# A list scheduler's cost table is refitted: attention and two MLPs in one kernel, same operations, another order

## The chip, the cores and the metric

The kernel runs on one core of a Trainium2 chip. The metric is the device time of one execution in microseconds (us), lower is better; the times shown are medians over several runs. A core has a matrix engine (TensorE, PE in the rows; PEld is its loading of weights), VectorE (DVE), ScalarE (ACT), GpSimd (POOL) and SyncE (SP). Here SP does nothing but issue transfers (DMA) between the chip's memory and the core.

## The reference

Three stages follow one another, with the output of each the input of the next. All tensors are fp32.

```python
# attention: q, k, v are (4, 8, 576, 64); window = 64
scores = scale * q @ k^T;  where not (0 <= pos_q - pos_k < window): -1e9
attn = exp(scores - max);  attn = attn / (sum + 1e-9);  out = attn @ v
x = out as 2304 tokens x 512
# first MLP: w_in (512, 2048), w_out (2048, 512), s and b scalars
r = max(x @ w_in, 0);  x = (s * r * r + b) @ w_out
# second MLP: w_in, w_out of the same sizes, alpha (2048,)
h = x @ w_in;  out = (max(h, 0) + alpha * min(h, 0)) @ w_out
```

## The kernel before, in words

Every fp32 matrix is split into a high and a low half, which PE multiplies as fp32r; one product costs three passes (high-high, high-low, low-high). Tokens lie along the columns.

In the opening, attention runs over groups of heads, block of tokens by block: scores on PE (L488, L500), mask and row maximum on DVE (L525), exponentials on ACT (L539), the sum's reciprocal on DVE (L549, L550), the normalising multiply on POOL (L557) or DVE, transposes (L574) and the product with v (L605) on PE. Between the groups, PE works on the first six of the first MLP's sixteen slices of 128 hidden units (L1075 in, L1135 out; 512 columns each). Later groups of heads lie beside that work, up to about 150 us.

The rest of the first MLP and all of the second work on pairs of slices and on thirds of the tokens, two halves of 384 columns, by a scheme with seven products in place of eight. Such a pair takes 90 matmuls of 384 columns: the products into the hidden units are L945, those out of them L1158. Copies of partial sums on ACT (L956) and one add on DVE (L973) stand between the L945 products; then comes the activation (ACT L1022 and L1026 in the first MLP, L1041 and L1042 with DVE L1045 in the second), the cast to the high half (ACT L1010 or DVE L1011) and the low half (DVE L1015). DVE adds the result onto the output (L1207).

The tokens' seven combinations (the X tiles, 768 KB each) are kept in the chip's memory and loaded for every turn by SP (L911). A weight slice is loaded by SP (L640, 512 KB), and prepared: two steps on ACT (L644, L648), five instructions on DVE (L653, L654, L658, L663 and the low half L675 or L711), the high half on ACT or DVE (L670, L672, L708). Three buffers hold loaded slices. The weight pairs' combinations are stored by SP (L758, wd<-ag) and loaded again for later turns (L779, aw<-wd).

No order is written out by hand. A class `Plan` collects 3475 steps, each with one or more ways (an engine, a cost in us, a function, a tail), the steps that it depends on and a due time `at`; some have an earliest time `after`. The method `emit` is a list scheduler that runs when the program is built: it keeps a time at which each engine comes free, computes for each ready step the earliest start (the end of what it depends on, plus `hop`, a cost for the change of engine), takes the earliest, and then among those of the same engine that could start then the one with the earliest due time:

```python
value = t + w[1] * (1.0 + self.SPARE[w[0]]) + w[3]   # the way taken is the one with the least
t0, i0, b0 = min(cands, key=lambda c: (c[0], self.steps[c[1]][2], c[1]))
```

So the costs decide two things: the order in which the steps stand on each engine, and, for steps with several ways, the engine. On the chip each engine runs its row in order, and waits for what its next instruction needs. Due times are worked out from absolute figures and from `PAIR`, the time of one pair of slices; `HURRY` (12 us) and `AHEAD` (30 us) set how far in front of its use a step is due or may begin.

Of the kernel before, what the change touches and what calls it, by code (L numbers as in the profile page):

```python
# [9 lines left out]
F32 = mybir.dt.float32  # L10
# [14 lines left out]
HALF = 384  # L25
# [43 lines left out]
class Plan:  # L69
# [93 lines left out]
    def emit(self):  # L163
# [67 lines left out]
def tile_window_attention_two_mlps(  # L231
# [78 lines left out]
    def dma(n, nbytes, fn):  # L310
        return [("sp", max(n * 0.45, nbytes / 380e3), fn, 2.0)]
# [18 lines left out]
    PAIR = 90 * (0.0137 + HALF * 0.00041)  # L330
# [5 lines left out]
    with tc.manual_schedule():  # L336
# [92 lines left out]
        def group(gi, bi, hps, at1, at2):  # L429
# [44 lines left out]
            def before():  # L474
# [30 lines left out]
                for t in range(len(hps)):  # L505
                    T.step([("pe", 0.25 + np_ * 0.23, lambda t=t: scores(t), 0.0)], reads=[(qk_, t)], writes=sc, at=at1)
# [37 lines left out]
                for h in range(2):  # L544
                    T.step([("act", 0.39 * NP, lambda h=h: exps(h), 0.1)], reads=[nm] + (sc if summed else [sm]),
# [6 lines left out]
                T.step([("dve", 0.36, inverse, 0.0)], writes=[(den, 0), (den, 1)], at=at1)  # L552
# [12 lines left out]
            def after():  # L565
# [10 lines left out]
                for h in range(2):  # L576
                    T.step([("pe", 0.05 + NP * 0.109, lambda h=h: transposes(h), 0.0)],
# [32 lines left out]
                for t in range(len(hps)):  # L610
                    T.step([("pe", 0.3 / len(hps) + 0.118 * u, lambda t=t: values(t), 0.0)],
# [18 lines left out]
        def converted(layer, f, part, at, after):  # L630
# [13 lines left out]
                [act(512, lambda: nc.scalar.activation(T[t], H().bitcast(F32), AF.Abs, scale=65536.0))],  # L644
# [3 lines left out]
                [act(512, lambda: nc.scalar.activation(L(), L().bitcast(U32), AF.Copy, scale=2.0 ** -29))],  # L648
# [7 lines left out]
            T.step([("dve", 0.8, exponent, 0.0, True)], writes=[t], at=at, after=after)  # L656
# [704 lines left out]
```

## Time and profile before

| | us |
|---|---|
| median of 3 runs | 852.15 |
| lowest, highest | 851.51, 853.44 |
| the profiled execution, device time | 854.11 |
| its span in the trace | 852.3 |
| PE busy | 832.7 |
| DVE busy | 651.1 |
| ACT busy | 510.5 |
| POOL busy | 103.5 |

A span is the time from the first to the last instruction in the trace; the device time of the same execution is 1.81 us longer. The busy time of an engine is the sum of its instructions' times. Idle time of an engine that isn't the bottleneck costs nothing by itself; it matters where the busiest engine waits for it.

### The profile page before, as it was taken

How to read it: one execution, taken by the hardware profiler on the slowest of the kernel's cores; microseconds unless marked ns; L12 is line 12 of the kernel's file. 1: busy time of each engine (PE TensorE's matmuls, PEld its weight loads, DVE VectorE, ACT ScalarE, POOL GpSimd, SP SyncE). 2: the span in 40 equal slices, each digit the busy share in tenths (PEclk: the TensorE clock that was granted, in tenths of full speed). 3: DMA queues.
4: the chain of work that ended last, by engine and by line, in shares of the span. 5: the costliest groups of instructions: out<-in, count | busy, mean ns of one | idle time of the engine just before them, and what ended most of it. 6: DMA issues, size and time to landing. Idle time of an engine off the chain costs nothing.

```text
span 852.3 us, 14883 instructions
## 1 busy us (share of the span) xinstructions
PE 832.7 (98%) x5556; PEld 787.7 (92%) x5556; DVE 651.1 (76%) x1175; ACT 510.5 (60%) x1217; POOL 103.5 (12%) x113
## 2 busy tenths in 40 slices
PE   7799999999999999999999999999999999999997
PEld 4678788888899999899999999999999999999997
DVE  6878799797997794699588989867767975864554
ACT  6878997545676474466365667655554754543431
POOL 6543344432100010011000000000000000000000
PEclk9999999999999999999999999999999999999999
DMA  8676973567578979957689359629774769435822
GB/s 282 195 214 179 297 229 111 209 218 275 202 253 316 406 243 363 380 189 305 225 319 340 131 214 354 239 75 346 259 252 156 243 254 348 144 110 187 295 76 75
DMA packets 65592, 202.57 MB, mean 238 GB/s; under 512 B 6640, under 2 KB 25072, under 8 KB 65520
## 3 DMA queue, kind: packets, MB, share of 16 engines
q1 hardware_dynamic: 65520, 201.62, 66.5%
q8 instruction: 44, 0.72, 0.3%
q14 instruction: 28, 0.23, 0.1%
HBM read 143.66 MB, written 57.93 MB: 237 GB/s over the span
## 4 chain that ended last, share of the span: by engine, by line
PE 88%; DMA 5%; ACT 2%; POOL 2%; DVE 1%; issue 1%; SPq 0%; DVEq 0%; POOLq 0%; ACTq 0%
PE y L1158 38%; PE h L945 18%; PE ab L945 13%; PE h L1075 9%; PE y L1135 4%; PE y L605 2%; DMA wd<-ag 2%; DMA raw<-w_out 2%; PE y L574 2%; PE ab L500 1%; DMA raw<-w_in 1%; POOL as__89 L557 1%; ACT as__89 L539 1%; PE ab L1158 0%; PE h L1158 0%
## 5 line engine op out<-in xcount | busy, mean ns | idle before, releaser
L1158 PE MATMUL y<-ax,woh 128*128 128x384 f32 x1216 | 275.4, 334 | 0.4 <-DVE ay L1207 0.4
L1158 PEld LDWEIGHTS y<-ax,woh 128*128 128x128 f32 x1216 | 216.3, 188 | 1.2 <-DVE ay L1207 0.9
L945 PE MATMUL h<-ax,aw 128*128 128x384 f32 x936 | 185.3, 335 | 0.3 <-ACT r L1022 0.2
L1158 PE MATMUL y<-ax,wol 128*128 128x384 f32 x608 | 169.4, 334 | 0.0
L945 PEld LDWEIGHTS h<-ax,aw 128*128 128x128 f32 x936 | 164.2, 188 | 1.4 <-ACT r L1022 0.6
L945 PE MATMUL ab<-ax,aw 128*128 128x384 f32 x702 | 140.4, 335 | 2.0 <-ACT h L956 1.5
L945 PEld LDWEIGHTS ab<-ax,aw 128*128 128x128 f32 x702 | 123.1, 188 | 2.9 <-ACT h L956 1.8
L1158 PEld LDWEIGHTS y<-ax,wol 128*128 128x128 f32 x608 | 111.1, 188 | 0.0
L1015 DVE TENSOR_TENSOR ax<-r,ax 128x384 fp32r<-128x384 f32 x156 | 86.2, 559 | 9.6 <-ACT ax L1010 7.5
L1207 DVE TENSOR_TENSOR ay<-y,ay 128x384 f32<-128x384 f32 x116 | 60.3, 552 | 38.5 <-PE y L1158 38.4
L1075 PE MATMUL h<-ax,aw 128*128 128x512 f32 (+1 forms) x360 | 85.1, 380 | 0.8 <-DVE ax L623 0.6
L1075 PEld LDWEIGHTS h<-ax,aw 128*128 128x128 f32 x360 | 62.8, 192 | 12.9 <-DVE ax L623 1.0
L1045 DVE SCALAR_TENSOR_TENSOR r<-aq,nalpha,r 128x384 f32<-128x384 f32 x96 | 58.5, 613 | 19.6 <-ACT aq L1042 16.6
L644 ACT ACTIVATE wt<-raw 128x512 f32<-128x512 f32 x64 | 43.3, 678 | 37.1 <-DMA raw<-w_out 16.3
L973 DVE TENSOR_TENSOR aq<-ab,aq 128x768 f32<-128x768 f32 x39 | 37.3, 956 | 31.1 <-PE ab L945 29.1
L1010 ACT CAST ax<-r 128x384 fp32r<-128x384 f32 x83 | 42.6, 514 | 25.9 <-DVE r L1045 23.7
L1041 ACT ACTIVATE r<-aq 128x384 f32<-128x384 f32 x48 | 24.8, 517 | 45.8 <-DVE aq L973 45.8
L658 DVE SCALAR_TENSOR_TENSOR raw<-raw 128x512 int32<-128x512 int32 x64 | 47.1, 738 | 1.8 <-ACT raw L648 1.8
L1026 ACT ACTIVATE r<-r 128x384 f32<-128x384 f32 (+2 forms) x90 | 47.5, 542 | 1.1
L557 POOL TENSOR_TENSOR as__89<-as__89,den 128x512 f32<-128x512 f32 x36 | 40.6, 1148 | 56.2 <-DVE den L550 43.7
L648 ACT ACTIVATE raw<-raw 128x512 int32<-128x512 uint32 x64 | 42.9, 679 | 5.7 <-DMA raw<-w_in 4.2
L663 DVE CUSTOM_DVE_ANT_0 wt<-raw,wt 128x1024 uint16<-128x1024 uint16 x64 | 45.0, 706 | 0.5
(140 smaller groups left out, 1149.9 us busy)
## 6 DMA issues: line engine op xcount, KB each, us to landing
ax<-xd SPq DMA_DIRECT2D x91, 768.0 KB, 6.9
wd<-ag SPq DMA_DIRECT2D x33, 512.0 KB, 8.0
aw<-wd SPq DMA_DIRECT2D x33, 512.0 KB, 5.0
raw<-w_in SPq DMA_DIRECT2D x32, 512.0 KB, 5.3
raw<-w_out SPq DMA_DIRECT2D x32, 512.0 KB, 6.4
xd<-ax SPq DMA_DIRECT2D x21, 768.0 KB, 4.3
xd<-aq SPq DMA_DIRECT2D x12, 768.0 KB, 4.1
xd<-ax SPq DMA_DIRECT2D x36, 192.0 KB, 4.6
```

What stands on the lines that cost most here:

```text
L557: eng.tensor_mul(x, x, d)
L644: [act(512, lambda: nc.scalar.activation(T[t], H().bitcast(F32), AF.Abs, scale=65536.0))],
L648: [act(512, lambda: nc.scalar.activation(L(), L().bitcast(U32), AF.Copy, scale=2.0 ** -29))],
L658: [dve(512, lambda: nc.vector.scalar_tensor_tensor(out=L(), in0=H(), scalar=-0x80000000, in1=L(), op0=ALU.bitwise_and, op1=ALU.bitwise_or) ...
L663: [dve(512, lambda: nc.vector.tensor_tensor(ti(), ti(), L(), op=ALU.add), port=True)],
L945: nc.tensor.matmul(bank(), W[:, wj, a, kt * P:(kt + 1) * P], X[:, c, kt, :], start=start and kt == 0 and y == 0, stop=kt == 1 and y == 2, ...
L1015: [dve(n, lambda: nc.vector.tensor_sub(T[gl], rn(), f32(T[gh])), port=True)],
L1026: [act(n, lambda: nc.scalar.activation(rn(), rn(), AF.Square)), dve(n, lambda: nc.vector.tensor_mul(rn(), rn(), rn()), port=True)],
L1045: [dve(HALF, lambda: nc.vector.scalar_tensor_tensor(out=rn(), in0=r2n(), scalar=nalpha[:, f:f + 1], in1=rn(), op0=ALU.mult, op1=ALU.add), ...
L1075: nc.tensor.matmul(T[ps][:, :n].rearrange("p (c t) -> p c t", t=P), T[w][:, k * P:(k + 1) * P], T[X(x, k)], start=st, stop=sp,)
L1158: nc.tensor.matmul(ps, T[w][:, m * P:(m + 1) * P], T[x], start=(i == 0 and j == 0), stop=(last and j == 2),)
L1207: ways = [dve(n, lambda a=a, yn=yn: nc.vector.tensor_add(a(), yn(), a()))]
```

## The change: the figures of the scheduler's table

The diff replaces numbers only. `hop` becomes 0.03 us within an engine (0.12 before), 0.2 from PE, 0.1 to POOL and 0.05 otherwise (before: 0.2 whenever PE is one of the two, else 0.1). The helper costs get a smaller fixed part and a tail, which counts for the next step but doesn't occupy the engine. A DMA is reckoned at its bytes over 410 GB/s (380 before; at least 0.45 us for each transfer, as before) and 2.6 us more until it has landed (2.0 before). `PAIR` goes from 15.40 to 15.60 us.

```diff
             if a == b:
-                return 0.0 if a == "pe" else 0.12
-            return 0.2 if "pe" in (a, b) else 0.1
+                return 0.0 if a == "pe" else 0.03
+            return 0.2 if a == "pe" else 0.1 if b == "pool" else 0.05
...
     def pe(n, cols, fn):
-        return [("pe", n * (0.0137 + cols * 0.000417), fn, 0.0)]
+        return [("pe", n * (0.0133 + cols * 0.0004167), fn, 0.0)]
 
-    def act(cols, fn):
-        return ("act", 0.2 + cols * 0.00084, fn, 0.0)
+    def act(cols, fn, fixed=0.065):
+        return ("act", fixed + cols * 0.00082, fn, 0.095)
 
-    def dve(cols, fn, fast=False, port=False):
-        return ("dve", 0.15 + cols * (0.00053 if fast else 0.00106), fn, 0.0) + (True,) * (fast or port)
+    def dve(cols, fn, fast=False, port=False, fixed=0.065):
+        return ("dve", fixed + cols * (0.00053 if fast else 0.00105), fn, 0.085) + (True,) * (fast or port)
...
     def dma(n, nbytes, fn):
-        return [("sp", max(n * 0.45, nbytes / 380e3), fn, 2.0)]
+        return [("sp", max(n * 0.45, nbytes / 410e3), fn, 2.6)]
...
-    PAIR = 90 * (0.0137 + HALF * 0.00041)
+    PAIR = 90 * 0.1733
```

Some twenty further figures, of single steps, are replaced in the same way: the cost of mask, maximum, exponentials, reciprocal, transposes and value products of the attention, of the weights' exponent step and sums, and the fixed part of some activations. No step, dependency, due-time constant or buffer is changed. The order of the engines' rows follows from the figures. On PE 754 of its 1039 steps keep their place, the others move by at most 16 places, and the last steps from about 847 us on stand as they did.

Transfers of layer one, from about 320 to 350 us. SP's row before; wd<-ag are stores of weight combinations, ax<-xd the X loads, raw the weight loads:

```order
L911 DMA ax<-xd 128x1536
L640 DMA raw<-w_in 128x1024
L911 DMA ax<-xd 128x1536 x7
L758 DMA wd<-ag 128x1024
L911 DMA ax<-xd 128x1536 x6
L758 DMA wd<-ag 128x512
L758 DMA wd<-ag 128x1024 x2
L640 DMA raw<-w_in 128x1024
L640 DMA raw<-w_out 128x1024 x2
L758 DMA wd<-ag 128x1024
```

SP's row at the same place after:

```order
L911 DMA ax<-xd 128x1536
L758 DMA wd<-ag 128x1024
L911 DMA ax<-xd 128x1536 x6
L758 DMA wd<-ag 128x512
L911 DMA ax<-xd 128x1536
L758 DMA wd<-ag 128x1024
L911 DMA ax<-xd 128x1536 x4
L758 DMA wd<-ag 128x1024
L911 DMA ax<-xd 128x1536 x2
L640 DMA raw<-w_in 128x1024 x2
L640 DMA raw<-w_out 128x1024
```

The stores have come forward among the X loads, and one weight load that stood in front of them now stands behind, next to the other.

ACT's row at about 353 to 361 us, before; the copies h<-ab and ab<-ab (L956) feed PE's next products, L644 and L648 begin the preparation of a weight slice:

```order
L1026 ACTIVATE r<-r 128x384
L1010 CAST ax<-r 128x384
L644 ACTIVATE wt<-raw 128x512
L648 ACTIVATE raw<-raw 128x512
L956 COPY h<-ab 128x384
L644 ACTIVATE wt<-raw 128x512
L648 ACTIVATE raw<-raw 128x512 x2
L1022 ACTIVATE r<-aq 128x384 x2
```

And after:

```order
L956 COPY ab<-ab 128x384
L644 ACTIVATE wt<-raw 128x512
L1022 ACTIVATE r<-h 128x384
L648 ACTIVATE raw<-raw 128x512
L1026 ACTIVATE r<-r 128x384
L644 ACTIVATE wt<-raw 128x512
L648 ACTIVATE raw<-raw 128x512
L644 ACTIVATE wt<-raw 128x512
L956 COPY h<-ab 128x384
L648 ACTIVATE raw<-raw 128x512
L708 ACTIVATE woh_4031<-wt,s_sb 128x512
L1022 ACTIVATE r<-aq 128x384 x2
```

Before the copy h<-ab there are now three of L644 and two of L648, where one of each stood.

DVE's row at about 236 to 246 us, before; L1184 adds results onto the output, L973 makes what the next activation reads:

```order
L1184 TENSOR_TENSOR ay<-y_2702,ay 128x512
L1184 TENSOR_TENSOR ay<-y_2708,ay 128x512
L1184 TENSOR_TENSOR ay<-y_2714,ay 128x512
L711 SCALAR_TENSOR_TENSOR wol_2819<-wt,s_sb,woh_2794 128x512
L653 TENSOR_SCALAR wt<-wt 128x512
L654 TENSOR_SCALAR wt<-wt 128x512
L1011 CAST ax<-r 128x384
L973 TENSOR_TENSOR aq<-ab,aq 128x768
L1015 TENSOR_TENSOR ax<-r,ax 128x384
L658 SCALAR_TENSOR_TENSOR raw<-raw 128x512
L653 TENSOR_SCALAR wt<-wt 128x512
L654 TENSOR_SCALAR wt<-wt 128x512
```

And after:

```order
L1184 TENSOR_TENSOR ay<-y_2715,ay 128x512
L675 TENSOR_TENSOR ag<-wt,ag 128x2x256
L1184 TENSOR_TENSOR ay<-y_2722,ay 128x512
L1184 TENSOR_TENSOR ay<-y_2732,ay 128x512
L653 TENSOR_SCALAR wt<-wt 128x512
L654 TENSOR_SCALAR wt<-wt 128x512
L658 SCALAR_TENSOR_TENSOR raw<-raw 128x512
L1011 CAST ax<-r 128x384
L663 ISA wt<-raw,wt 128x1024
L1015 TENSOR_TENSOR ax<-r,ax 128x384
L973 TENSOR_TENSOR aq<-ab,aq 128x768
```

Three preparation steps (L675, L658, L663) and one low half (L1015) more stand in front of L973 now, and L711 is no longer there.

ACT's row at about 628 to 635 us, before; the four on aq are the relus of one pair of slices:

```order
L1010 CAST ax<-r 128x384
L956 COPY h<-ab 128x384
L644 ACTIVATE wt<-raw 128x512
L648 ACTIVATE raw<-raw 128x512
L670 CAST woh_7583<-wt 128x512
L644 ACTIVATE wt<-raw 128x512
L648 ACTIVATE raw<-raw 128x512
L1041 ACTIVATE r<-aq 128x384
L1042 ACTIVATE aq<-aq 128x384
L1041 ACTIVATE r<-aq 128x384
L1042 ACTIVATE aq<-aq 128x384
L956 COPY ab<-h 128x384
```

And after:

```order
L956 COPY h<-ab 128x384
L1041 ACTIVATE r<-aq 128x384
L1042 ACTIVATE aq<-aq 128x384
L1041 ACTIVATE r<-aq 128x384
L1042 ACTIVATE aq<-aq 128x384
L1042 ACTIVATE aq<-h 128x384
L644 ACTIVATE wt<-raw 128x512
L1010 CAST ax<-r 128x384
L1041 ACTIVATE r<-h 128x384
L956 COPY ab<-h 128x384
L648 ACTIVATE raw<-raw 128x512
L1010 CAST ax<-r 128x384
```

The preparation steps that stood in front of the four relus are behind them, one L644 excepted, which is still in front of copy ab<-h.

## Rows read from the trace of the kernel before

**Rows 1.** The page: busy time, and the granted clock in 40 slices.

```profile
PE 832.7 (98%) x5556; PEld 787.7 (92%) x5556; DVE 651.1 (76%) x1175; ACT 510.5 (60%) x1217; POOL 103.5 (12%) x113
...
PEclk9999999999999999999999999999999999999999
```

**Rows 2.** Busy time (us and count) of each engine in stretches, clock, DMA share, GB/s.

```profile
0.00:60.00 60.00, 47.79 (x637) 36.35 (x638) 46.45 (x84) 45.09 (x173) 31.02 (x54) 0.94 0.71 229
250.00:400.00 150.00, 147.83 (x851) 146.41 (x850) 117.53 (x233) 91.17 (x189) 9.60 (x7) 1.00 0.86 324
400.00:830.00 430.00, 429.47 (x2476) 428.75 (x2475) 314.06 (x590) 236.78 (x504) 0.00 (x0) 1.00 0.62 227
38.00:40.00 2.00, 2.00 (x21) 1.88 (x18) 1.44 (x4) 1.89 (x12) 0.00 (x0) 0.50 0.18 23
105.00:150.00 45.00, 45.00 (x400) 36.24 (x399) 42.56 (x60) 36.41 (x97) 20.34 (x17) 1.00 0.61 181
205.00:245.00 40.00, 39.97 (x190) 34.18 (x189) 38.32 (x70) 25.93 (x47) 4.58 (x3) 1.00 0.52 177
```

**Rows 3.** PE's waits: us in total, times, longest.

```profile
PE y L574 <- POOL as__89 L557: 6.4, 3, 4.2
...
PE ab L945 <- ACT h L956: 1.5, 1, 1.5
...
PE ab L945 <- ACT ab L956: 0.5, 1, 0.5
...
PE y L1158 <- DVE ay L1207: 0.4, 1, 0.4
PE h L945 <- ACT r L1022: 0.2, 1, 0.2
```

**Rows 4.** Chain of waits from 326 to 343 us: start, length, what.

```profile
332.66 7.81 DMA wd<-ag
...
340.49 0.43 DVE ag L672
```

**Rows 5.** Chain of waits from 344 to 361 us.

```profile
347.48 11.21 DMA raw<-w_in
...
358.71 0.66 ACT wt L644
359.37 0.57 ACT raw L648
359.94 0.39 ACT h L956
```

**Rows 6.** SP's timeline from 320 to 370 us: start, length of issue.

```profile
345.85 1.57 SPq L758 DMA_DIRECT2D wd<-ag  x3
```

**Rows 7.** ACT's timeline from 627 to 637 us, idle time before in brackets.

```profile
629.94 0.66 ACT L644 ACTIVATE wt<-raw 128x512 f32<-128x512 f32 x1 [3.40 <-DMA raw<-w_out]
...
632.73 0.53 ACT L1041 ACTIVATE r<-aq 128x384 f32<-128x384 f32 x1
```

**Rows 8.** DVE's timeline from 234 to 248 us.

```profile
238.80 0.74 DVE L711 SCALAR_TENSOR_TENSOR wol<-wt,s_sb,woh 128x512 fp32r<-128x512 f32 x1
...
241.39 0.55 DVE L1015 TENSOR_TENSOR ax<-r,ax 128x384 fp32r<-128x384 f32 x1
241.86 0.69 DVE L658 SCALAR_TENSOR_TENSOR raw<-raw 128x512 int32<-128x512 int32 x1
242.46 0.42 DVE L653 TENSOR_SCALAR wt<-wt 128x512 f32<-128x512 f32 x1
...
243.53 0.69 DVE L663 CUSTOM_DVE_ANT_0 wt<-raw,wt 128x1024 uint16<-128x1024 uint16 x1
...
246.27 0.69 DVE L675 TENSOR_TENSOR ag<-wt,ag 128x512 fp32r<-128x512 f32 x1
```

**Rows 9.** PE's timeline from 26 to 36 us.

```profile
34.36 0.66 PE L574 MATMUL y<-ident,as__89 128*128 128x128 f32 x4 [1.40 <-POOL as__89 L557]
35.80 0.44 PE L574 MATMUL y<-ident,as__89 128*128 128x128 f32 x2 [0.79 <-POOL as__89 L557]
```

More of the change, by code (lines that the diff above doesn't have):

```diff
@@ L505, in before @@
                 for t in range(len(hps)):
-                    T.step([("pe", 0.25 + np_ * 0.23, lambda t=t: scores(t), 0.0)], reads=[(qk_, t)], writes=sc, at=at1)
+                    T.step([("pe", 0.12 + np_ * 0.23, lambda t=t: scores(t), 0.0)], reads=[(qk_, t)], writes=sc, at=at1)
                 x0 = next(x for x in range(len(ROW)) if ROW[x:x + np_] == pairs)
@@ L529, in before @@
                 if not summed:
-                    T.step([("dve", 0.1 + FULL * 0.00108, mask, 0.0)], reads=sc + capped, writes=[sm], at=at1)
+                    T.step([("dve", 0.06 + FULL * 0.00105, mask, 0.085)], reads=sc + capped, writes=[sm], at=at1)
                 T.step(
-                    [("dve", (0.4 if summed else 0.12) + FULL * 0.00106, top, 0.0)],
+                    [("dve", (0.32 if summed else 0.06) + FULL * 0.00105, top, 0.085)],
                     reads=sc if summed else [sm], writes=[nm], at=at1,
@@ L544, in before @@
                 for h in range(2):
[L545 removed]
+                    T.step([("act", (0.345 if summed else 0.388) * NP, lambda h=h: exps(h), 0.06)], reads=[nm] + (sc if summed else [sm]),
                            writes=[(sm, h), (den, h)], at=at1)
@@ L550, in inverse @@
                     nc.vector.reciprocal(T[den], T[den])
-                T.step([("dve", 0.36, inverse, 0.0)], writes=[(den, 0), (den, 1)], at=at1)
+                T.step([("dve", 0.32, inverse, 0.085)], writes=[(den, 0), (den, 1)], at=at1)
                 def norm(eng, h):
@@ L576, in after @@
                 for h in range(2):
-                    T.step([("pe", 0.05 + NP * 0.109, lambda h=h: transposes(h), 0.0)],
+                    T.step([("pe", 0.04 + NP * 0.09, lambda h=h: transposes(h), 0.0)],
                            reads=["ident", (sm, h)], writes=[pp[h]], at=at2)
@@ L610, in after @@
                 for t in range(len(hps)):
-                    T.step([("pe", 0.3 / len(hps) + 0.118 * u, lambda t=t: values(t), 0.0)],
+                    T.step([("pe", 0.24 / len(hps) + 0.118 * u, lambda t=t: values(t), 0.0)],
                            reads=[(vt, t)] + pt, writes=[(av[0], t)], at=at2)
@@ L654, in exponent @@
                 nc.vector.tensor_scalar(ti(), ti(), 3, None, op0=ALU.logical_shift_left)
-            T.step([("dve", 0.8, exponent, 0.0, True)], writes=[t], at=at, after=after)
+            T.step([("dve", 0.79, exponent, 0.085, True)], writes=[t], at=at, after=after)
             T.step(
@@ L762, in weight_pair @@
             stage(0, lambda: x3(T[ts[0]]), [ts[0]])
-            T.step([("dve", 1.75, adds, 0.0, True)], reads=ts, writes=[sums_], at=at, after=after)
+            T.step([("dve", 1.47, adds, 0.085, True)], reads=ts, writes=[sums_], at=at, after=after)
             stage(1, lambda: x3(a(1, 1)), [ts[1]])
@@ L1021, in squared @@
             rn = lambda: T[r][:, :n]
-            T.step([act(n, lambda: nc.scalar.activation(rn(), hn(), AF.Relu)),
+            T.step([act(n, lambda: nc.scalar.activation(rn(), hn(), AF.Relu), 0.1),
                     dve(n, lambda: nc.vector.tensor_scalar_max(rn(), hn(), 0.0))],
@@ L1040, in lrelu @@
             rn, r2n = (lambda: T[r][:, :HALF]), (lambda: T[r2])
-            T.step([act(HALF, lambda: nc.scalar.activation(rn(), hn(), AF.Relu))], reads=[hk], writes=[r], at=at - HURRY)
-            T.step([act(HALF, lambda: nc.scalar.activation(r2n(), hn(), AF.Relu, scale=-1.0))],
+            T.step([act(HALF, lambda: nc.scalar.activation(rn(), hn(), AF.Relu), 0.1)], reads=[hk], writes=[r], at=at - HURRY)
+            T.step([act(HALF, lambda: nc.scalar.activation(r2n(), hn(), AF.Relu, scale=-1.0), 0.1)],
                    reads=[hk], writes=[r2], at=at - HURRY)
```

14 lines of the change are left out of this document (7 added, 7 removed).

## The prediction, on record before the changed kernel was run

> **What bounds the kernel now.** I read the page first, then the stretches, then PE's waits, then the chain and the timelines at each wait. The page shows PE busy in 832.7 of 852.3 us, at nine tenths or more of the full granted clock in all 40 slices [rows 1]; the change alters no operation, so nothing in those 832.7 us can go, and all that it can move is the 19.6 us in which PE stands still, or the same kind of time newly made. The stretches say where these are [rows 2]: 12.2 us before 60 us, 2.2 us from 250 to 400, 0.5 us from 400 to 830. From 60 to 250 there is almost none (PE 45.00 of 45 from 105 to 150, 39.97 of 40 from 205 to 245); the tail after 830 keeps its order of PE work, and I leave it alone. PE's waits name the releasers [rows 3]: POOL's normalising multiply (L557) 6.4 us in three waits, all in the opening; ACT's copy h (L956) 1.5 us; ACT's copy ab 0.5 us; DVE's add L1207 0.4 us; ACT's relu 0.2 us. DVE is the engine nearest to becoming the bound: 42.56 of 45 us at 105 to 150, and 38.32 of 40 at 205 to 245 [rows 2]. Those two stretches hide whatever the new order does badly, or fail to.
>
> The profiled execution took 854.11 us: span 852.3 and 1.81 around it. The sum below is made against it; the median of the three runs, 852.15, lies 1.96 below, and I carry that difference over unchanged.
>
> **The change, part by part.** No cost here is an instruction's cost: each term is a wait that goes or comes because something stands elsewhere in a queue.
>
> (a) 290 to 345 us, SP. Before, the weight store wd that frees what DVE's L672 writes next was issued behind seven X loads at 332.66 and took 7.81 us to land [rows 4]; L672, and behind it the add L1207 for which PE waits 0.4 us [rows 3], could not start earlier. In the new row of SP the store stands behind the first X load, seven loads sooner. A load of 768 KB takes 2.1 us at the rate of that stretch (324 GB/s at a share of 0.86, so 377 GB/s when busy [rows 2]), so seven are worth up to 14 us where 0.4 are needed. The wait of 0.2 us on ACT's relu in the same stretch has a wait for a weight load in front of it, and the loads there come some issues earlier too. Together -0.6 us; between -0.6 and 0 (the store could be held by its own data instead).
>
> (b) 345 to 400 us, SP and ACT. Before, ACT's copy h stood behind two steps of weight preparation (L644, 0.66 us, and L648, 0.57 us), which waited for a weight load issued at 347.48 and landed 11.21 us later, at 358.69 [rows 5]. The copy ran at 359.94 and PE lost 1.5 us [rows 3], so it was wanted by 358.4. Now the first load of the group is one that used to stand in front of the X burst and has moved behind it; five steps of preparation, of three loads, stand ahead of copy h. When do they land? At the latest 1.4 us sooner than before, at 357.3: the same bytes are in front but for one 512 KB load (512 KB at 377 GB/s are 1.4 us). At the earliest another 3.5 us sooner, at 353.8, since the three stores (1.3 MB) that were issued at 345.85 [rows 6] have gone ahead of the X loads. I take the middle, 355.5; the other two loads follow 1.4 us apart, at 356.9 and 358.3. Behind the third there is L644 and then the copy: 358.9, or 0.5 us late; since the first L644 also stands ahead of a relu that feeds PE's y products, I take 1.0 us for the new waits. With the earliest landing they are 0, with the latest 2.3 (357.3 + 2.8 + 0.6 - 358.4). So the term is -1.5 + 1.0 = -0.5 us, between -1.5 and +0.8.
>
> The trace's row for such a load is 11.21 us from issue to landing [rows 5]. The Trainium skill, DMA: Bandwidth & Descriptors, Anatomy of one DMA, gives a single transfer (on GpSimd's path) about 2.0 us plus its bytes over 436 GB/s, an estimate of 3.2 us for 512 KB. By that rule the moved loads would land near 349 us, no new wait would come, and this term would be -1.5 and the sum 1.0 us lower. The row disagrees by 8 us, because these transfers queue behind thirteen others; the measurement decides.
>
> (c) 634 us, ACT. Before, ACT waited 3.40 us for a load up to 629.94 [rows 7], and then ran a copy and two pairs of preparation steps before the four relus (L1041, L1042) and copy ab; PE lost 0.5 us [rows 3]. Now the four relus and the copy stand ahead of all but one of these steps. The relus read what DVE's L973 had written by 632.4, and ACT began them at 632.73 [rows 7]: 0.3 of the 0.5 us comes back by ACT's order alone, the rest if L973, which stood behind two steps of the same preparation, comes forward with it. I take -0.5 us; 0 if the four relus are late for another reason.
>
> (d) 225 to 250 us, DVE. The new row has L675, L658, L663 and L1015 ahead of the add L973 that feeds PE, and L711 no longer: 0.69 + 0.69 + 0.69 + 0.55 - 0.74 = 1.9 us more [rows 8]. What covers it is DVE's idle time in 205 to 245, 40 - 38.32 = 1.7 us [rows 2]. I take the difference, +0.2; if none of the idle time lies in front of L973, +1.9; if PE's products have slack, 0. Before showed no wait here.
>
> (e) 90 to 150 us, SP, ACT and DVE. Three weight loads of the first layer stand two to four issues later, behind loads of v and stores of x. So the preparation of two weight tiles, five DVE steps each (0.42 twice and 0.69 three times, 2.9 us [rows 8]), is pushed towards the stretch in which DVE has 45 - 42.56 = 2.4 us free [rows 2]. If both fall wholly into it: 5.8 - 2.4 = +3.4 us. If the load's start moves but the work still fits: 0. Before has no wait there at all, PE being 45.00 of 45, so I take a value near the lower end, +0.6.
>
> (f) Opening, up to 60 us. Some choices among POOL, DVE and ACT flip (over the whole program DVE has 11 steps fewer, ACT 12 more, POOL 1 fewer, and these swaps run beside PE). One half of an early normalising multiply goes from POOL to DVE; a cast of 0.6 us comes ahead of exponentials on ACT; PE's transposes and value products change places. Two of POOL's waits (1.40 and 0.79 us [rows 9]) come from multiplies that run one after the other on POOL. Followed by hand, the exponentials that gate the next groups end within 0.6 us of where they did, some before, some after. I take -0.3 us. The bounds: both of these waits gone and the half clock after the second (PE at 0.50 in 38 to 40 [rows 2], some 3.4 us long at half speed, so 1.7 us) gone too, -3.9; the cast and one DVE step of 0.69 us both on the path, +1.3.
>
> Sum: -0.6 - 0.5 - 0.5 + 0.2 + 0.6 - 0.3 = -1.1 us. Profiled 854.1 would become 853.0, and the median 851.0. All lower ends together give -6.5, all upper ends +7.4.
>
> **Rivals.**
> A, slower: weight preparation ahead of urgent work. One mechanism: the refitted figures for DVE are smaller (0.065 + tail where 0.15 stood), the list believes DVE sooner free and lets preparation in front of L973 or of the attention's casts. It decides from the point where the work added in front exceeds DVE's idle time, 2.4 us in 105 to 150 and 1.7 in 205 to 245. For it: DVE's 95% in both stretches. Against: the order moves mostly by a few places, and the new figures lie nearer to the rows. Price: (e) and (d) at their upper ends, (b) as taken, the rest as it is: -0.6 - 0.5 - 0.5 + 1.9 + 3.4 - 0.3 = +3.4, so 855.5.
> B, clearly faster: the opening. If the normalising multiplies on two engines end early enough, the two waits and the half-clock stretch go, -3.9 in place of -0.3, with (d) and (e) at nothing: -3.9 - 1.6 = -5.5; with half of the opening's gain -3.6. I take -4.2, so 848.0. For it: 12.2 us of idle time lie there; against: the three waits hang on a chain of exponentials that no figure shortens.
> C, the new order is hidden: waits go as in (a) to (c) but the same loads make new ones a few steps on. PE's total stays, 852.
>
> **How the numbers follow.** The forecast, 851.0, has a chance of 0.42 and a range of its own of 848.8 to 853.3 (terms (b) and (e) each off by 1 to 1.5). A has 0.25 (853.9 to 859), B 0.24 (845.6 to 850.4), C 0.09. A measurement of this kernel tells 0.2%, 1.7 us, from no change: faster is below 850.4, slower above 853.9. The forecast's 0.42 splits into 0.16 faster, 0.25 same and 0.01 slower; B adds 0.24 to faster, C 0.09 to same, A 0.25 to slower: 0.40, 0.34, 0.26. The range 847.0 to 856.0 cuts the lower third of B and the upper third of A.
>
> **What would show it.** In the profile after: PE idle in 250 to 400 falls from 2.2 to about 1.1 us, with the wait on copy h at 1.0 or below, none on L1207, and none at 634; at 345 us the weight load lands between 354 and 357. If (d) is wrong, PE waits over 0.5 us for DVE's L973 or what follows it between 240 and 250; if (e) is, PE falls below 44 of 45 us in 105 to 150. If the opening's idle time leaves 11 to 13 us, (f) is wrong. A new wait of over 1.5 us from 400 to 830, where I foresee none, would upset the whole reading.

## The result: slower by 1.5%, and the profile after

The changed kernel took 865.4 us (median of 4 runs, 864.78 to 866.46) against 852.8 of the kernel before: a ratio of 1.0146, 95% interval 1.0130 to 1.0162. The forecast was 851.0 with a range to 856; the nearest rival, A, stood at 855.5. The span of the profiled execution grew from 852.3 to 863.0, by 10.7 us, while the work stayed what it was. First the page's line of busy times, to be read against [rows 1]:

```profile
PE 836.4 (97%) x5552; PEld 785.7 (91%) x5556; DVE 647.0 (75%) x1164; ACT 514.5 (60%) x1229; POOL 101.0 (12%) x112
```

PE stands still for 863.0 - 836.4 = 26.6 us in place of 19.6, and is busy 3.7 us longer by this line, in which the ends of matmuls are modelled. By stretches, with columns as in [rows 2]; PE's idle time is the first figure less the second:

```profile
0.00:60.00 60.00, 45.99 (x629) 34.59 (x634) 45.63 (x81) 45.44 (x172) 28.62 (x53) 0.94 0.70 230
60.00:105.00 45.00, 45.00 (x604) 36.16 (x603) 32.22 (x51) 38.46 (x141) 15.01 (x15) 1.00 0.68 199
105.00:150.00 45.00, 42.52 (x389) 33.51 (x388) 43.66 (x63) 38.09 (x105) 22.30 (x17) 1.00 0.66 206
...
225.00:262.00 37.00, 33.99 (x174) 30.57 (x173) 34.69 (x63) 25.14 (x51) 4.26 (x3) 1.00 0.50 184
250.00:400.00 150.00, 146.79 (x829) 143.15 (x830) 112.97 (x220) 90.70 (x187) 9.56 (x7) 1.00 0.83 311
400.00:830.00 430.00, 428.99 (x2465) 426.39 (x2466) 310.07 (x583) 239.99 (x516) 0.00 (x0) 1.00 0.63 233
```

Two stretches that the rows of before did not have, for comparison, of the kernel before:

```profile
60.00:105.00 45.00, 45.00 (x605) 36.52 (x604) 35.16 (x55) 40.18 (x147) 16.15 (x16) 1.00 0.78 235
...
225.00:262.00 37.00, 36.97 (x201) 34.99 (x200) 32.94 (x62) 24.75 (x50) 5.87 (x4) 1.00 0.65 237
```

In the opening, PE's idle time goes from 12.2 to 14.0 us. About 0.6 us of the 14.0 is no real idle time: four of the opening's matmuls (the second of a pair on L488) have no record in the trace after. From 60 to 105 DVE does 32.22 us of work where it did 35.16, in four instructions fewer; from 105 to 150 it does 43.66 of 45 us where it did 42.56 [rows 2], in three more, and PE stands still for 2.48 us where it had no idle time at all. From 225 to 262 PE loses 3.01 us (before 0.03). From 250 to 400 it is 3.2 in place of 2.2, from 400 to 830 1.0 in place of 0.5. PE's waits, to be read against [rows 3]:

```profile
PE y L574 <- POOL caps L350: 4.7, 1, 4.7
PE h L945 <- ACT h L956: 2.1, 2, 1.5
PE y L605 <- ACT ay L581: 2.0, 4, 0.9
PE h L1075 <- DVE ax L623: 1.6, 2, 1.4
...
PE y L574 <- DVE ax L623: 1.1, 2, 0.6
PE y L574 <- POOL as__89 L557: 1.0, 2, 0.5
PE ab L945 <- ACT ab L956: 0.8, 1, 0.8
PE ab L945 <- ACT h L956: 0.8, 1, 0.8
...
PE y L1158 <- DVE ay L1207: 0.7, 1, 0.7
```

Two of the expected waits are gone: that on ACT's copy ab at 634 us (the 0.8 us of the row above stand at 250), and L1207's 0.4 us at 341 (the 0.7 us stand at 365). The waits on POOL's normalising multiply (L557) fell from 6.4 to 1.0 us, but the first transpose still waits 4.7 us, put down to POOL's caps now, and those on ACT's L581 went from 0.4 to 2.0 us. The largest new ones are at 243 us on copies h and ab (L956), and from 124 to 140 on DVE's L623.

To see how the difference grows I compare, in both traces, the start of the weight load that belongs to the same matmul by its count (all 5538 are recorded in both, 18 small ones left out):

| weight load no. | start before | later after by |
|---|---|---|
| 840 | 75.2 us | 1.5 us |
| 1440 | 121.4 | 0.4 |
| 1680 | 157.8 | 3.9 |
| 2040 | 234.8 | 3.9 |
| 2160 | 256.4 | 7.6 |
| 2400 | 298.1 | 8.8 |
| 2940 | 395.9 | 9.0 |
| 3600 | 510.3 | 11.6 |
| 4200 | 614.3 | 12.1 |
| 4380 | 646.5 | 11.1 |
| 5520 | 844.2 | 11.1 |

So the loss has four places: the opening (0.4 us by this count, 1.2 by idle time), 121 to 158 (3.5), 235 to 256 (3.7), and 396 to 510 (2.6), with one more of 1.2 us up to 298. What was forecast as a gain, the wait at 634, came: 12.1 to 11.1.

How do 3.7 us come about at 243? ACT's timeline there, after:

```profile
241.91 0.62 ACT L670 CAST ag<-wt 128x512 fp32r<-128x512 f32 x1 [2.17 <-DVE wt L663]
242.44 0.68 ACT L644 ACTIVATE wt<-raw 128x512 f32<-128x512 f32 x1
243.02 0.66 ACT L648 ACTIVATE raw<-raw 128x512 int32<-128x512 uint32 x1
243.58 0.46 ACT L1022 ACTIVATE r<-h 128x384 f32<-128x384 f32 x1
...
244.51 0.47 ACT L956 COPY h<-ab 128x384 f32<-128x384 f32 x1
```

ACT stands still for 2.17 us ahead of L670, waiting for DVE's L663. Behind L670, in ACT's row, come two preparation steps, the two activation steps L1022 and L1026, and then copy h, for which PE waits 1.5 us. What stands in the way is not the length of L670 (0.62 us) but the time until its input is there. Before, ACT's row had a wait of the same kind at this place, and it did no harm, since its input came early enough and copy h still had to wait 0.43 us for PE:

```profile
236.52 0.72 ACT L708 ACTIVATE woh<-wt,s_sb 128x512 fp32r<-128x512 f32 x1 [2.22 <-DVE wt L663]
```

After, one more such step, L670, stands ahead of copy h, and DVE is late with its input:

```profile
238.61 1.41 DVE L654 TENSOR_SCALAR wt<-wt 128x512 int32<-128x512 int32 x1
...
241.20 0.68 DVE L663 CUSTOM_DVE_ANT_0 wt<-raw,wt 128x1024 uint16<-128x1024 uint16 x1
...
247.53 0.95 DVE L973 TENSOR_TENSOR aq<-ab,aq 128x768 f32<-128x768 f32 x1
```

L654 took 1.41 us where 0.43 is usual; POOL's L705 ran beside it. The row ran without a gap from 229 us, and L973 came at 247.5; before, at 240.5. With PE 3.9 us late on arrival, that is 3.1 us of its own. Before, too, DVE had no gap from 222.5 to 241 us, and two steps that ran longer beside POOL (L1015 1.78 us at 228, L653 1.52 at 233); PE had no wait from it.

### The profile page after: what moved, and what is told of

It reads as the page before. It is cut to its first block, busy times and chain, and to the rows that moved or that the text cites. A ratio compares the mean times of both kernels' runs of the same rounds, so it can differ in the third digit from the quotient of the medians.

```text
span 863.0 us, 14912 instructions
## 1 busy us (share of the span) xinstructions
PE 836.4 (97%) x5552; PEld 785.7 (91%) x5556; DVE 647.0 (75%) x1164; ACT 514.5 (60%) x1229; POOL 101.0 (12%) x112
## 4 chain that ended last, share of the span: by engine, by line
PE 78%; DVE 12%; DMA 4%; ACT 3%; issue 2%; POOL 1%; SPq 0%; DVEq 0%; POOLq 0%; ACTq 0%
PE y L1158 35%; PE h L945 16%; PE ab L945 12%; PE h L1075 7%; PE y L1135 3%; DMA raw<-w_in 3%; DVE raw L658 2%; PE ab L500 1%; DVE wt L653 1%; DVE wt L663 1%; PE y L605 1%; PE y L574 1%; DVE ay L1207 1%; DMA raw<-w_out 1%; DVE wt L654 1%
## 5 line engine op out<-in xcount | busy, mean ns | idle before, releaser
L945 PE MATMUL h<-ax,aw 128*128 128x384 f32 x936 | 188.2, 336 | 3.2 <-ACT h L956 2.1
L1207 DVE TENSOR_TENSOR ay<-y,ay 128x384 f32<-128x384 f32 x116 | 60.9, 550 | 42.9 <-PE y L1158 42.9
L1015 DVE TENSOR_TENSOR ax<-r,ax 128x384 fp32r<-128x384 f32 x156 | 86.2, 559 | 2.9 <-ACT ax L1010 0.7
L973 DVE TENSOR_TENSOR aq<-ab,aq 128x768 f32<-128x768 f32 x39 | 37.2, 953 | 41.5 <-PE ab L945 41.3
L644 ACT ACTIVATE wt<-raw 128x512 f32<-128x512 f32 x64 | 42.9, 672 | 29.1 <-DMA raw<-w_in 16.3
L1026 ACT ACTIVATE r<-r 128x384 f32<-128x384 f32 (+2 forms) x90 | 47.3, 541 | 1.6 <-DVE r L1023 0.6
L658 DVE SCALAR_TENSOR_TENSOR raw<-raw 128x512 int32<-128x512 int32 x64 | 47.4, 746 | 0.1
L557 POOL TENSOR_TENSOR as__89<-as__89,den 128x512 f32<-128x512 f32 x35 | 39.9, 1160 | 63.8 <-DVE den L550 50.0
L1022 ACT ACTIVATE r<-h 128x384 f32<-128x384 f32 (+2 forms) x56 | 28.8, 514 | 30.0 <-PE h L1075 20.3
L663 DVE CUSTOM_DVE_ANT_0 wt<-raw,wt 128x1024 uint16<-128x1024 uint16 x64 | 46.1, 721 | 0.4
```

The source lines that it names most:

```text
L557: eng.tensor_mul(x, x, d)
L658: [dve(512, lambda: nc.vector.scalar_tensor_tensor(out=L(), in0=H(), scalar=-0x80000000, in1=L(), op0=ALU.bitwise_and, op1=ALU.bitwise_or) ...
L663: [dve(512, lambda: nc.vector.tensor_tensor(ti(), ti(), L(), op=ALU.add), port=True)],
L945: nc.tensor.matmul(bank(), W[:, wj, a, kt * P:(kt + 1) * P], X[:, c, kt, :], start=start and kt == 0 and y == 0, stop=kt == 1 and y == 2, ...
L1015: [dve(n, lambda: nc.vector.tensor_sub(T[gl], rn(), f32(T[gh])), port=True)],
L1026: [act(n, lambda: nc.scalar.activation(rn(), rn(), AF.Square), 0.1), dve(n, lambda: nc.vector.tensor_mul(rn(), rn(), rn()), port=True)],
```

## Experiments

Theory 1: DVE's new figures are too low, and let preparation in front. Theory 2: the old order is an unusually good one, and any other costs 5 to 20 us, whichever figure is changed. Theory 3: the fault lies in PE's figures of the opening. Theory 4: figures below what the chip takes let it fall behind the plan, and the order is made for a state that doesn't come. Theory 5: at 243 us preparation stands ahead of urgent steps, and moving it cures this. Theory 6: contention of DVE with POOL's adds, which neither table contains in full.

**Is the loss local?** The list's result can be written out as a row of steps, so that two orders can be joined. The steps are the same in both tables, and any first part of the one can be followed by the rest of the other.

In words:

```diff
-            t0, i0, b0 = min(cands, key=lambda c: (c[0], self.steps[c[1]][2], c[1]))
+            i0, eng = the next of a written row of 3475 steps
```

> A row of steps written out: the first 653 steps in the old order (up to about 160 us), the rest in the changed one. If each loss is local to its place: 865.4 less the 4.6 us that the changed order had lost by 158 us, 860 to 861.5. If the loss at 243 us is the DVE backlog that the changed order brings along from before 160 us: 856.5 to 858.

> The other way round: the first 653 steps in the changed order, the rest in the old one. If each loss is local to its place: 852.8 plus 4.6, 857 to 858. If a backlog is carried on: 860 to 863.

Measured: 861.56 us (ratio to before 1.0098, 1.0078 to 1.0118) and 857.78 us (1.0047, 1.0029 to 1.0066). The stretches of the first and of the second, 105 to 150 and 225 to 262 us:

```profile
105.00:150.00 45.00, 45.00 (x401) 36.33 (x401) 41.77 (x59) 35.82 (x97) 20.32 (x18) 1.00 0.60 181
225.00:262.00 37.00, 33.84 (x179) 31.16 (x179) 30.72 (x55) 21.48 (x46) 4.25 (x3) 1.00 0.55 204
```

```profile
105.00:150.00 45.00, 42.53 (x389) 33.53 (x388) 43.66 (x63) 38.10 (x105) 22.27 (x17) 1.00 0.66 205
225.00:262.00 37.00, 36.64 (x194) 34.00 (x192) 33.61 (x61) 26.82 (x53) 5.53 (x4) 1.00 0.56 207
```

Each half has its own loss and not the other's: 3.16 us of idle time at 225 to 262 in the first, 2.47 at 105 to 150 in the second. Over their before the two lost 8.4 and 4.7 us, together 13.1, as against 12.6 for the whole. The losses are local and add up; no backlog is carried from 150 to 243.

**Which figures?** Each of four groups was put back alone in the changed table, for instance for DVE:

```diff
-        return ("dve", fixed + cols * (0.00053 if fast else 0.00105), fn, 0.085) + (True,) * (fast or port)
+        return ("dve", 0.15 + cols * (0.00053 if fast else 0.00106), fn, 0.0) + (True,) * (fast or port)
```

> The changed table with DVE's figures alone put back (0.15 us fixed, no tail, the old mask, maximum, reciprocal, exponent and sums). Theory 1 (the new DVE figures believe DVE free too soon, and preparation of weights gets in front of what PE waits for, from 105 to 150 and at 243 us): these two losses, 2.9 and 3.5 us, mostly go, 857 to 860. Theory 2 (no one group is at fault; any new order of this finely balanced kernel costs some 5 to 15 us): 858 to 870, with new waits at other places. Theory 3 (the loss comes from the figures of PE in the opening, DVE's are harmless): 864 to 866.

> The changed table with ACT's figures alone put back (0.2 us fixed, no tail, the old exponentials). Theory 1 (DVE's figures): little comes back, 862 to 866. Theory 2 (any order costs something): 858 to 870. Theory 4 (a plan that runs ahead of the chip on whichever engine costs by as much as it runs ahead; this table's plan ends at 845.4 us where the changed one's ends at 840.5 and the old one's at 851.3): about half of the loss back, 858 to 860.

> The changed table with PE's figures alone put back (the matmul's cost and those of scores, transposes and value products). Its plan ends at 848.0 us, 7.6 later than with the changed table. Theory 1 (DVE's figures): the matmul figures are the same within 0.3%, the losses at 105 to 150 and 243 us stay, 861 to 866. Theory 3 (the opening's PE figures start the lag of the chip behind the plan): most comes back, 853 to 858. Theory 4 (the gap between plan and chip as a whole): 855 to 859.

> The changed table with the hop costs alone put back (0.12 within an engine, 0.2 with PE on either side, else 0.1). Its plan ends at 842.6 us. Theory 1 (DVE's figures): a hop of 0.12 us within DVE lengthens each chain of preparation steps, so a third of the loss comes back, 860 to 864. Theory 2 (any order costs something): 858 to 870. Theory 4 (the gap between plan and chip): 862 to 865.

Measured: DVE 863.31 us (ratio 1.0113, 1.0084 to 1.0143), ACT 871.23 (1.0202, 1.0172 to 1.0231), PE 872.39 (1.0221, 1.0190 to 1.0252), hop 863.81 (1.0116, 1.0086 to 1.0146). No group alone brings the time back; putting back ACT's or PE's makes it slower still, and theory 3 falls. The figures of POOL and of DMA, and PAIR, were not put back alone.

Putting back DVE's figures brings 2 to 3 us, not 6. But the two losses that theory 1 named did mostly go, which the median hides. The stretches and the longest wait behind them with DVE's figures put back:

```profile
105.00:150.00 45.00, 44.56 (x400) 35.98 (x400) 38.06 (x60) 38.57 (x106) 18.64 (x15) 1.00 0.61 188
225.00:262.00 37.00, 36.06 (x191) 33.31 (x190) 33.14 (x60) 27.26 (x57) 4.36 (x3) 1.00 0.68 255
```

```profile
504.55 1.90 PE L945 MATMUL ab<-ax,aw 128*128 128x384 f32 x5 [2.22 <-DVE ax L675]
```

PE's idle time is 0.44 and 0.94 us in place of 2.48 and 3.01. By the count of weight loads this order is only 1.1 us late at 158 us, 3.3 at 256 and 2.7 at 486 (the changed one 3.9, 7.6 and 11.2). Then one wait of 2.22 us at 504, with a granted clock of 0.62 from 505 to 509 behind it, makes 4.4 us. So theory 1 is right on the two places and wrong on the total. That DVE's figures are the fault isn't shown by it either: half a per cent on the changed table, below, also leaves only 0.3 us at 158. Undoing one group of such a table turns out to be no way of finding its fault: each undoing gives another order.

**Contention beside POOL.** In the changed order from 105 to 150 us, DVE's and POOL's timelines:

```profile
134.37 0.69 DVE L1015 TENSOR_TENSOR ag<-r,ag 128x512 fp32r<-128x512 f32 x1
134.97 1.79 DVE L658 SCALAR_TENSOR_TENSOR raw<-raw 128x512 int32<-128x512 int32 x1
136.68 1.50 DVE L711 SCALAR_TENSOR_TENSOR wol<-wt,s_sb,woh 128x512 fp32r<-128x512 f32 x1
138.10 1.50 DVE L663 CUSTOM_DVE_ANT_0 wt<-raw,wt 128x1024 uint16<-128x1024 uint16 x1
```

```profile
134.53 1.67 POOL L705 TENSOR_TENSOR wsum<-wsum,wt 128x512 f32<-128x512 f32 x1 [2.96 <-DVE wt L663]
136.17 2.88 POOL L843 TENSOR_TENSOR as__89<-ax 128x384 f32<-128x384 f32 x2
```

L1015, which began before POOL's add, takes 0.69 us; after it, beside POOL's adds, L658, L711 and L663 take 1.5 to 1.8. (The Trainium skill, SBUF — State Buffer, Who interferes with whom, has VectorE and GpSimd share one pair of ports that one of them holds for a whole instruction; these rows agree, at 0.8 to 1.1 us for each instruction met.) Both tables do hold a term for this: the list lengthens a DVE step marked as sharing by 0.8 of its overlap with the POOL step that it has running. In the changed table that is at most 0.5 us for a step of 512 columns, and L705 is reckoned at 1.0 us where it took 1.67 here. So the term is too small, not absent. To take the contention away and leave every row of steps as it stands, POOL's adds were cut to 8 columns; the sums that they make are left out of the output.

```diff
-                    nc.gpsimd.tensor_add(wsum, wsum, T[t])
+                    nc.gpsimd.tensor_add(wsum[:, :8], wsum[:, :8], T[t][:, :8])
...
-                    eng.tensor_add(x4(t)[:, k], part(0, r, c)[:, k], part(1, r, c)[:, k])
+                    eng.tensor_add(*(z[:, :, :8] if eng is nc.gpsimd else z for z in (x4(t)[:, k], ...)))
```

> The changed order, with POOL's adds of wsum (L705) and of the X combinations (L843) cut to 8 columns of each row, so that these parts of the output are left out; every row of steps stands as it did. Theory 6 (no figure of either table contains that DVE's two-input instructions take about 1.5 us in place of 0.69 beside POOL's adds; this puts DVE late from 105 to 150 and at 243 us): most of the 2.9 and 3.5 us comes back, 859 to 861.5. If the order alone is late: 864 to 866.

> The old order, with POOL's adds of wsum and of the X combinations cut to 8 columns as in new_less_pool (these parts of the output are left out). Theory 6 (contention beside POOL): DVE gains the same time, but the old order had it covered, PE having no wait from 60 to 240 us, so 851.5 to 853. If cutting POOL's adds helps whatever the order: 846 to 849.

Measured: 859.16 us in the changed order (ratio 1.0068, 1.0051 to 1.0085), 851.72 in the old (0.9992, 0.9979 to 1.0005). The changed one's stretches:

```profile
105.00:150.00 45.00, 44.77 (x401) 35.93 (x400) 40.55 (x66) 38.24 (x103) 13.96 (x19) 1.00 0.68 215
225.00:262.00 37.00, 35.84 (x193) 33.63 (x192) 28.97 (x58) 23.80 (x49) 0.97 (x3) 1.00 0.62 225
```

and two instructions of DVE in it:

```profile
238.95 0.43 DVE L654 TENSOR_SCALAR wt<-wt 128x512 int32<-128x512 int32 x1
...
241.23 0.95 DVE L973 TENSOR_TENSOR aq<-ab,aq 128x768 f32<-128x768 f32 x1
```

PE's idle time from 105 to 150 falls from 2.48 to 0.23 us, and at 225 to 262 from 3.01 to 1.16. The same row of DVE reaches L973 at 241.2 where it was 247.5 (PE is 4.3 us earlier there, DVE 6.3). The old order gains 1.1 us at most from the same cut, the changed one 6.2. So about 5 of the 12.6 us come with POOL's adds, and the old order had them covered: theory 6 holds for 105 to 158 and for more than half of 243. The cut also ends POOL's own steps sooner; what that gives isn't told apart from the contention. The other 7.4 us (859.16 against 851.72) are there without POOL's adds; by the count of weight loads, 4.0 of them arise between 256 and 486 us.

**Preparation moved at 243.** In the written row, the preparation of two weight slices was pushed behind what is urgent, first behind L973 alone (12 steps), then behind the whole chain that follows it (17 steps). On DVE, the first, in words:

```diff
-L658, L663 (slice 10), L675, then L653, L654, L658, L663 (slice 11) ahead of L973
+L973, then L658, L663 (slice 10), L675, L653, L654, L658, L663 (slice 11)
```

> The changed order, written out, with one edit near 243 us: twelve preparation steps of two weight slices (and one store) stand behind the add L973 in place of ahead of it, on DVE and ACT. Theory 5 (what costs 3.5 us there is preparation standing ahead of the copy h, L956, and of L973): the waits of 1.5 and 0.9 us on these go, 862 to 863.7. If DVE is simply short of time there and something else is late at once: 864.5 to 866.

> The changed order, written out; the same preparation steps near 243 us (and those that follow from them, 17 in all) stand behind the whole urgent chain: L973, the two relus on aq, the copy into hb, and the two low halves L1015. Theory 5 (preparation ahead of urgent steps is what costs 3.5 us there): the waits of 1.5, 0.9 and 0.6 us go, 862 to 863.8, and no half clock. If DVE is short of time: 865 to 868 as in the first try.

Measured: 867.73 us (ratio 1.0179, 1.0158 to 1.0200) and 870.64 (1.0207, 1.0184 to 1.0230): slower than the changed kernel by 2.3 and 5.2 us. Theory 5 fails in this form. PE in the first and in the second:

```profile
253.08 2.29 PE L945 MATMUL ab<-ax,aw 128*128 128x384 f32 x6 [3.87 <-ACT ab L956]
```

```profile
255.57 2.29 PE L945 MATMUL h<-ax,aw 128*128 128x384 f32 x6 [5.10 <-ACT r L1022]
```

The urgent chain did run sooner (L973 at 244.8 and 243.9 in place of 247.5), and the wait of 1.5 us on copy h went down to 0.55 in both. The wait of 0.85 us on copy ab became the 3.87 us of the first run; in the second it went, and 5.10 us for a relu came twelve matmuls on. For the moved steps pass their results from DVE to ACT and back, and as one block they now stand ahead of the next urgent ones. The order before has them singly between urgent ones. With POOL's adds cut and nothing moved, the wait on copy h is 0.55 us too. So preparation ahead of copy h and the contention are shown to make most of the 1.5 us together; that another order cures the loss there isn't shown.

**Figures and the chip.** The whole table was multiplied where the list reads it, for DVE and ACT:

```diff
-                    w = w[:4]
+                    w = (w[0], w[1] * {"dve": 1.15, "act": 1.15}.get(w[0], 1.0), w[2], w[3])
```

> The changed table with DVE's and ACT's costs multiplied by 1.15 where the list reads them; nothing else. Its plan ends at 853.9 us. Theory 4 (a plan whose figures are below what the steps take on the chip, with their contention, lets the chip fall behind it, and the order is then made for a state that doesn't come): the chip keeps to this plan, 854 to 859. Theory 2 (any new order of this finely balanced kernel costs some 5 to 20 us): 858 to 872, and the chip far behind the plan.

> The old table with DVE's and ACT's costs multiplied by 0.995: a change that means nothing, and that still moves steps. Its plan ends at 852.5 us. Theory 4 (figures below the chip's): the chip keeps within 3 us of the plan, 852 to 856. Theory 2 (any new order costs): 858 to 868.

> The old table with PAIR alone changed, 15.40 to 15.60 us, so that due times of the pairs come later by 0.2 us for each pair. Its plan ends at 853.0 us. Theory 4 (figures below the chip's): 853 to 857, since no cost is lowered. Theory 2 (any new order costs): 858 to 868.

> The old table with DVE's and ACT's costs multiplied by 0.90, as far below the old as the refit puts them. Its plan ends at 846.5 us. Theory 4 (figures below the chip's): the chip falls 12 to 20 us behind the plan, 859 to 867. Theory 2 (any new order costs): 858 to 868, not told apart here. If neither holds: 851 to 856.

> The changed table with DVE's and ACT's costs times 1.10, POOL's per column 0.0024 in place of 0.00184, and its add of X combinations 2.4 us in place of 1.7, as the trace has them. Its plan ends at 848.6 us. Theory 4 (figures below the chip's are what costs): the chip keeps to the plan, 850 to 854. Theory 2 (the old order is an unusually good one, any other costs 5 to 20 us): 858 to 868.

> The old table with DVE's and ACT's costs times 1.005. Its plan ends at 853.9 us. Theory 2 (the old order is an unusually good draw): 857 to 864, like its other neighbour. Theory 4 (figures not below the chip's keep the plan): 853 to 856.

> The changed table with DVE's and ACT's costs times 1.005. Theory 2 (any order is a draw): anywhere from 857 to 872, and the losses at other places than the changed order's. If the refitted figures as such cost 12 us: 864 to 867, with losses at the same places.

The plan's end is the list's own forecast when the program is built; the chip's lag is the profiled span less that end.

| table | plan's end | lag | median, us | ratio to before |
|---|---|---|---|---|
| old | 851.3 | 1.0 | 852.8 | |
| old, times 1.005 | 853.9 | -1.7 | 854.12 | 1.0004 (0.9989 to 1.0020) |
| old, PAIR changed | 853.0 | 1.1 | 855.68 | 1.0031 (1.0015 to 1.0046) |
| old, times 0.995 | 852.5 | 6.3 | 859.88 | 1.0081 (1.0061 to 1.0100) |
| old, times 0.90 | 846.5 | 21.2 | 870.14 | 1.0204 (1.0183 to 1.0225) |
| new, times 1.15 | 853.9 | 9.2 | 867.25 | 1.0167 (1.0141 to 1.0192) |
| new, times 1.10, POOL's too | 848.6 | 17.7 | 866.47 | 1.0156 (1.0130 to 1.0181) |
| new | 840.5 | 22.5 | 865.4 | 1.0146 (1.0130 to 1.0162) |
| new, times 1.005 | 840.2 | 16.3 | 860.10 | 1.0078 (1.0064 to 1.0092) |
| new, DVE's put back | 845.3 | 15.3 | 863.31 | 1.0113 |
| new, ACT's put back | 845.4 | 25.5 | 871.23 | 1.0202 |
| new, PE's put back | 848.0 | 21.6 | 872.39 | 1.0221 |
| new, hop put back | 842.6 | 19.8 | 863.81 | 1.0116 |

Three things are to be seen. The refit took 10.8 us off the plan, and the chip then fell 22.5 us behind it, where from 50 us on it had kept within 2.5 us of the old plan. The old figures were above what steps take and so left room for contention: from 150 to 260 us of its own clock the old plan has 98.9 us of DVE's steps, and DVE was busy for 93.6 in the trace; the refitted plan has 88.8, and DVE was busy for 95.2. Lowering the old table by a tenth does the same as the refit (lag 21.2, 17 us lost), more than either theory forecast. But theory 4 fails twice. The old table times 0.995, with a plan that ends later than the old one, lost 7 us. And the other way: raising the new table does not bring the old time back, neither by 1.15 nor by 1.10 with POOL's figures put right (the chip lagged 17.7 us behind that plan). The second of these, by stretches:

```profile
0.00:60.00 60.00, 45.27 (x623) 34.18 (x627) 45.29 (x86) 42.78 (x163) 29.32 (x54) 0.91 0.70 223
105.00:150.00 45.00, 45.00 (x458) 36.36 (x457) 41.94 (x63) 39.48 (x113) 20.22 (x18) 1.00 0.69 211
...
262.00:400.00 138.00, 133.53 (x759) 130.93 (x758) 104.33 (x209) 81.09 (x167) 8.52 (x7) 1.00 0.84 311
```

With these figures 105 to 150 has no idle time any more, and the loss stands elsewhere: PE's idle time is 14.7 us in the opening (before 12.2) and 4.5 from 262 to 400 (2.2). And half a per cent, which means nothing, makes 5.3 us around the new table (860.10) and 7 us on one side of the old (859.88), none on the other (854.12). So theory 2 holds for a good part: of twelve other tables none gave an order better than the old, and the old and its neighbours by +0.5% and by PAIR are the only ones below 859. Those two neighbours (854.12 and 855.68) are also where its forecast of 857 or more failed. How much of the 7.4 us beside contention belongs to the refit as such, and how much to the draw, stays open: the two runs of the changed table, half a per cent apart, differ by 5.3 us.

**A joined order.** The first 300 us of the old order, the order of the table with PAIR changed to 420, the old to 590, the changed one to the end:

> A row of steps joined from three: the old order up to 300 us, that of the table with PAIR alone changed up to 420, the old up to 590, the changed one to the end. If gains and losses are local, as the two halves showed: -1.2 at 350 to 365 (PAIR's order) and -1.0 at 615 to 660 (the changed order), 850.5 to 851.5. If they hang on what went before: 852 to 854.

Measured: 851.94 us (ratio 0.9990, 0.9974 to 1.0005), not told apart from before. Its stretch from 262 to 400:

```profile
262.00:400.00 138.00, 137.33 (x789) 135.75 (x788) 109.87 (x219) 85.69 (x175) 8.30 (x6) 1.00 0.83 313
```

PE's idle time is 0.67 us there and 0.00 from 400 to 700, in place of 2.2 and 0.5; the waits did go, and 0.9 us of the median with them, within the interval.

## Why the prediction was wrong, by its steps

- (a), -0.6 us: wrong in sign, about +1.2 from 286 to 340. L1207's wait at 341 us went, as forecast. In place of the relu's 0.2 us a wait of 0.8 (1.1 at the weight load) for copy h came at 303, behind a weight load that landed 10.7 us after issue; the term had the loads there come sooner.
- (b), -0.5 us: its mechanism was right. The weight load landed at 363.7, which is about 355 on the clock of before (PE was 8 to 9 us later), between the 353.8 and 357.3 forecast and near the 355.5 taken. The chain there:

```profile
354.33 9.35 DMA raw<-w_in
...
365.29 0.93 DVE ay L1207 x2
```

  The new wait came on L1207, 0.7 us by the waits and 1.2 with the gap at 367, against 1.0 forecast. From 340 to 396 us the changed order neither gained nor lost (8.9 and 9.0 us late).
- (c), -0.5 us: right, about -1.0 at 615 to 647.
- (d), +0.2 us: mis-sized, it was 3.7. The step that failed is "What covers it is DVE's idle time in 205 to 245". Idle time summed over 40 us is no cover: DVE had no gap after 229 us, and in the trace of before, where this could have been read, none from 222.5 us to L973. And the price wasn't DVE's 1.9 us alone, my upper end: L973 came 3.1 us later against PE, and ACT's L670 stood ahead of copy h and waited for DVE. With POOL's adds cut, 1.3 of the 3.7 us remain.
- (e), +0.6 us: mis-sized, it was 2.5 by idle time and 3.5 by the count. I took a value near the lower end with the argument that PE had no wait there before, which says nothing once the cover is gone. That the upper end, 3.4, comes near is luck: it has ten preparation steps move into the stretch, and only two short ones did (one L653, one L654). From 60 to 150 us both traces have six each of L653, L654, L658 and L663. What grew is their length beside POOL, for instance L658's from 105 to 150, before and after (us in all, mean ns of one, idle time before):

```profile
L658 DVE SCALAR_TENSOR_TENSOR raw<-raw 128x512 int32<-128x512 int32 x6 | 5.0, 833 | 0.0
```

```profile
L658 DVE SCALAR_TENSOR_TENSOR raw<-raw 128x512 int32<-128x512 int32 x6 | 6.1, 1018 | 0.0
```

  With POOL's adds cut, 0.23 of the 2.48 us remain. The step that failed is the price: moved steps at 0.42 and 0.69 us each [rows 8], none of them made longer by POOL.
- (f), -0.3 us: wrong in sign, +1.2 by idle time (1.8 less the four missing records) and +0.4 by the count at 121 us. Two POOL waits went, as the rival B had it, and were replaced by waits for ACT's L581 (2.0 us in place of 0.4), DVE's L672 (0.7) and smaller ones, with 0.5 us more at the first transpose.
- No term stood for 396 to 510 us (2.6 us). These are new waits, in a stretch in which the trace of before had none, and so gave no row to price them by. PE's busy line shows 1.0 of them; the waits of its weight loads from 400 to 530 show most of the rest:

```profile
PEld h L945 <- ACT r L1022: 1.3, 4, 0.6
PEld h L945 <- ACT r L1041: 1.0, 1, 1.0
```

  The sign named for this, a new wait of over 1.5 us from 400 on, didn't come: the loss was in pieces of 1.0 us and less.
- Rival A named the two places, and for 243 us the mechanism; its price of 855.5 was 10 us short, since it counted DVE alone and left out what follows (ACT behind DVE, POOL beside it, places without a row). At 0.25 its chance was too low for another reason: I read each moved step for itself and did not ask what the order of before was worth. It had PE waiting for 0.03 us from 60 to 250, and it kept to its plan within 2.5 us. Chances to lose were many, to win few; the gains open to any order were the 3 us of waits that could be named, and they came in part.

## What to carry to other kernels

A table of costs in a list scheduler isn't only a set of durations: figures above the real ones hold room for contention and waits. That this room is what kept the old order good is argued here, not shown, since raising the new figures by 10 or 15% didn't bring the time back. Still, compare the plan's clock with the trace, place by place, before and after a refit, not only each figure with its instruction. Where the bottleneck engine already stands still for almost nothing, a re-ordering has little to win and the whole cover to lose: price such a change by the cover (each helper engine's idle time near the place, not over a stretch), and give a loss more than an even chance where its sign can't be shown; of twelve other tables none was faster here. And a step placed ahead of an urgent one costs the time until its input arrives, not its own length.

## What the runs showed of the hardware

When PE had stood still for 3.87 us in the run with preparation moved (PE's row above), its granted clock went to half for the next stretch. Stretches of that run, columns as in [rows 2], the clock third from the end:

```profile
253.00:257.00 4.00, 3.92 (x12) 3.92 (x13) 2.90 (x7) 2.90 (x7) 0.00 (x0) 0.50 0.35 107
257.00:261.00 4.00, 4.00 (x18) 4.00 (x18) 3.50 (x5) 2.11 (x4) 1.28 (x1) 0.72 0.96 330
261.00:265.00 4.00, 3.39 (x20) 3.07 (x19) 1.71 (x4) 2.47 (x6) 0.00 (x0) 1.00 0.90 327
```

The level was 0.50 from 253 to 257 us, mixed after that, and full again from 261; six matmuls took 2.29 us where they take 1.20 at full clock. In prep_behind the clock was 0.50 from 255 to 261 us, behind the wait of 5.10, and in undo_dve 0.62 from 505 to 509, behind one of 2.22. A wait of 1.47 us in the changed kernel at 243 us was followed by full clock (1.00 from 225 to 262). So these three waits cost PE twice, and part of what the three runs lost is this. And VectorE's contention with GpSimd reaches in-place operations with one input as well: L654 took 1.41 us beside L705 in the changed kernel (DVE's row above), where 0.43 is usual, and new_less_pool has it at 0.43 in the same place.
